# The feed-forward part on two 64-row TensorE tiles, with fences and block ends ordered by hand

## The chip, the cores and the metric

The kernel runs on one core of a Trainium2 chip. The metric is the device time of one execution in microseconds (us). A core has a matrix engine (TensorE, "PE" in the profile, with its weight loads as "PEld"), a vector engine (VectorE, "DVE"), an engine for activation functions (ScalarE, "ACT"), GpSimd ("POOL") and a queue engine that issues most transfers (SyncE, "SP"). They run side by side and wait for one another through semaphores. TensorE writes only to PSUM, eight banks of 128 partitions by 512 fp32 values here; ScalarE and VectorE read the results from there.

## What is computed

Inputs are bf16. There are 2048 tokens of width D = 576. A layernorm of x feeds two branches: a sliding-block attention (32 query heads, 16 key and value heads of width 128, the last 512 cached positions), and a mixer with a feed-forward network of width F = 4608. Cut to what matters:

```python
def _B_ref(x, w1, w2, w3, w4):
    h = _gelu(_layernorm(x, axis=-1) @ w1)
    ...
    hs = jnp.concatenate([g0, g1, g2, g3], axis=-1) @ w2
    x1 = x + hs
    h2 = _gelu(_layernorm(x1, axis=-1) @ w3) @ w4
    return x1 + h2

x = A_x
xn = _layernorm(x, axis=-1)
s = _A_ref(xn, A_k_cache, A_v_cache, A_wq, A_wo)
g = _silu(_B_ref(xn, B_w1, B_w2, B_w3, B_w4))
return x + s * g
```

The change touches the line of `h2` (the feed-forward part): `w3` is 576 x 4608, `w4` is 4608 x 576.

## The kernel before

Tokens are taken in NB = 4 blocks of QB = 512, each of TB = 4 row tiles of 128. The first part of the program (up to line 657) does the attention and the mixer for all blocks and leaves s and x1 in DRAM scratch. The second part, from line 660, is the feed-forward network; the layernorm of x1 for a block (`ln3_steps`, line 164) writes `xm_b`, and four DMA transposes (`ln3_transpose`, line 168) bring it, as `xT_b`, into the form that a matmul streams.

Weights are loaded once, in nine slices (`load_w`, line 679): `w3_s` with five chunks of 128 rows for the contraction over D = 4 x 128 + 64 (the fifth chunk holds 64 rows of weights and 64 of zeros, set by a memset on GpSimd, line 682), and `w4_s`. All of these loads stand on SP's queue, three for a slice, ahead of the loads of s and x (`load_sx`, line 694).

F is cut into FC = 36 columns of 128, called fc. `up(b, fc)` (line 703) runs five matmuls of 512 streamed columns, one for each chunk of D, into one PSUM bank `ph`, and a gelu on ScalarE (line 711) makes the bf16 tile `h3` of it. `down(fc, tt)` (line 714) multiplies one 128-token piece of `h3` with `w4`: 512 columns into the bank `pm[tt]` (line 717) and the last 64 into `pr` (line 718). PSUM has three banks for `ph`, four for `pm` and one for `pr`, which all four row tiles share.

Blocks 0 to 2 run ups and downs in turn, the downs LA = 3 fc behind the ups (loop at line 760). After the last down of a block, `finish` (line 721) adds x1 on VectorE (line 731), takes a tanh on ScalarE (line 733), forms out and g with four more VectorE operations (lines 735, 736, 738, 741) and stores them. Block 3 runs all its ups first, then the downs of one row tile after the other, the last of them in three cuts of columns (line 786), so that little is left behind the last matmul.

In this part the order on every engine comes from a scheduler that follows the program's order and priorities; only in the first part are SP, GpSimd and TensorE ordered by hand (`tc.manual_schedule`). Waits between engines and for the reuse of a buffer are placed automatically.

Of the kernel before, what the change touches and what calls it, by code (L numbers as in the profile page):

```python
# [8 lines left out]
P = 128  # L9
# [6 lines left out]
SP = mybir.EngineType.SP  # L16
POOL = mybir.EngineType.Pool
PE = mybir.EngineType.PE

LN_EPS = 1e-5  # L20
GELU_A = 0.7978845608028654
# [8 lines left out]
def kernel(  # L30
# [14 lines left out]
    nc = tc.nc  # L45
# [72 lines left out]
        nc.scalar.activation(out=e[:], in_=y[:, 0:1], func=ACT.Exp, scale=0.0)  # L118
        return y

    def layernorm_steps(pool, dsts, srcs, rsqrt=rsqrt_newton):
        n = len(srcs)
        hw = D // 2
        st_ = {}

        def stats(i):
            if i == 0:
                st_["mv"] = pool.tile([P, n, 2], FP32, name="ln_mv")
            st = pool.tile([P, 2, 6], FP32, name="ln_st")
            for j in range(2):  # L130
                tc.keep_in_program_order(
                    nc.vector.bn_stats(out=st[:, j, :], in_=srcs[i][:, j * hw:(j + 1) * hw]))
            nc.vector.bn_aggr(out=st_["mv"][:, i, :], in_=st[:])

        def inv():
            st_["r"] = rsqrt(pool, st_["mv"][:, :, 1], n)

        def apply(i):
            nc.vector.tensor_scalar(out=dsts[i], in0=srcs[i], scalar1=st_["mv"][:, i, 0:1],
                                    scalar2=st_["r"][:, i:i + 1], op0=ALU.subtract, op1=ALU.mult)  # L140

        return ([lambda i=i: stats(i) for i in range(n)] + [inv] + [lambda i=i: apply(i) for i in range(n)])

# [15 lines left out]
    def load_x1(b):  # L159
        x1 = x1_pool.tile([P, TB, D], BF16, name="x1")  # L160
        nc.sync.dma_start(out=x1[:], in_=rows(x1_dram, b * TB, TB))
        x1_t[b] = x1

    def ln3_steps(b):
        xm = xm_b[b % 2]
        return layernorm_steps(small, [xm[:, tt, 0:D] for tt in range(TB)], [x1_t[b][:, tt, :] for tt in range(TB)])

    def ln3_transpose(b):
        for tt in range(TB):
# [2 lines left out]
    with ExitStack() as actx:  # L172
        def pool(name, bufs, space=None):
            kw = {} if space is None else {"space": space}
            return actx.enter_context(tc.tile_pool(name=name, bufs=bufs, **kw))
# [484 lines left out]
    with ExitStack() as bctx:  # L660
# [4 lines left out]
        res = pool("b_res", 1)  # L665
        WS = 4
        NSL = FC // WS
        w3_s, w4_s = [], []
        for i in range(NSL):
            w3_s.append(res.tile([P, NDC, WS * P], BF16, name=f"w3_s{i}"))  # L670
            w4_s.append(res.tile([P, WS, D], BF16, name=f"w4_s{i}"))
        h3_pool = pool("h3_pool", 6)
        hl_pool = pool("hl_pool", FC)
        fin = pool("fin", 2)
        sx_pool = pool("sx_pool", 2)
        ps_h3 = pool("ps_h3", 3, PSUM)
        ps_h2 = pool("ps_h2", 1, PSUM)

        def load_w(i):
            w3, w4 = w3_s[i], w4_s[i]  # L680
            c0 = i * WS * P
            nc.gpsimd.memset(w3[DR:, NF, :], 0.0)
            nc.sync.dma_start(out=w3[:, 0:NF, :],
                              in_=B_w3[0:NF * P, c0:c0 + WS * P].rearrange("(kc p) f -> p kc f", p=P))
            nc.sync.dma_start(out=w3[0:DR, NF, :], in_=B_w3[NF * P:D, c0:c0 + WS * P])
            nc.sync.dma_start(out=w4[:], in_=B_w4[c0:c0 + WS * P, :].rearrange("(fc p) d -> p fc d", p=P))

        with tc.issue_after(last_t[0].ins):
            for i in range(NSL):
# [4 lines left out]
        def load_sx(b):  # L694
            s_b = sx_pool.tile([P, TB, D], BF16, name="s_b")
            nc.sync.dma_start(out=s_b[:], in_=rows(s_dram, b * TB, TB))
            x_b = sx_pool.tile([P, TB, D], BF16, name="x_b")
            nc.sync.dma_start(out=x_b[:], in_=rows(x2, b * TB, TB))
            sx_t[b] = (s_b, x_b)

        h3_t = {}

        def up(b, fc, hp):
            ph = ps_h3.tile([P, QB], FP32, name="ph3", tag="h3")
            w3 = w3_s[fc // WS]
            f0 = (fc % WS) * P
            for kc in range(NDC):
                nc.tensor.matmul(ph[:, :], lhsT=w3[:, kc, f0:f0 + P], rhs=xT_b[b % 2][:, kc, :],  # L708
                                 start=(kc == 0), stop=(kc == NDC - 1))
            h3 = hp.tile([P, QB], BF16, name="h3")  # L710
            nc.scalar.activation(out=h3[:, :], in_=ph[:, :], func=ACT.Gelu_apprx_tanh)  # L711
            h3_t[fc] = h3

        def down(pm, pr, fc, tt):
            w4 = w4_s[fc // WS]
            lhsT = h3_t[fc][:, tt * P:(tt + 1) * P]
            nc.tensor.matmul(pm[tt][:, :], lhsT=lhsT, rhs=w4[:, fc % WS, 0:M0], start=(fc == 0), stop=(fc == FC - 1))  # L717
            nc.tensor.matmul(pr[:, tt, :], lhsT=lhsT, rhs=w4[:, fc % WS, M0:D],  # L718
                             start=(fc == 0 and tt == 0), stop=(fc == FC - 1), skip_group_check=True)

        def finish(b, tt, parts):
            t = b * TB + tt
            s_b, x_b = sx_t[b]
            o = fin.tile([P, D], BF16, name="o")
            g2 = fin.tile([P, D], BF16, name="g2")

            def part(ps, lo, hi):
                n = hi - lo
                bs = fin.tile([P, n], FP32, name="bs")
                for src, l0, l1 in ps:  # L730
                    nc.vector.tensor_tensor(out=bs[:, l0 - lo:l1 - lo], in0=src, in1=x1_t[b][:, tt, l0:l1], op=ALU.add)  # L731
                th = fin.tile([P, n], FP32, name="th")
                nc.scalar.activation(out=th[:], in_=bs[:], func=ACT.Tanh, scale=0.5)
                t1 = fin.tile([P, n], FP32, name="t1")
                nc.vector.tensor_tensor(out=t1[:], in0=bs[:], in1=s_b[:, tt, lo:hi], op=ALU.mult)
                nc.vector.scalar_tensor_tensor(out=o[:, lo:hi], in0=th[:], scalar=1.0, in1=t1[:], op0=ALU.add,
                                               op1=ALU.mult)
                nc.vector.tensor_tensor(out=o[:, lo:hi], in0=o[:, lo:hi], in1=x_b[:, tt, lo:hi], op=ALU.add)
                if hi == D:
                    nc.sync.dma_start(out=out2[t * P:(t + 1) * P, :], in_=o[:])  # L740
                nc.vector.scalar_tensor_tensor(out=g2[:, lo:hi], in0=th[:], scalar=1.0, in1=bs[:], op0=ALU.add,
                                               op1=ALU.mult)
                if hi == D:
                    nc.scalar.dma_start(out=g_dram[t * P:(t + 1) * P, :], in_=g2[:])

            for ps, lo, hi in parts:
                part(ps, lo, hi)
            return part

        LA = 3  # L750
        for b in range(NB):
            load_sx(b)
            lastb = b == NB - 1
            if not lastb:
                load_x1(b + 1)
            pm = [ps_h2.tile([P, M0], FP32, name=f"pm{tt}") for tt in range(TB)]
            pr = ps_h2.tile([P, TB, R0], FP32, name="pr")
            whole = lambda tt: [([(pm[tt][:, :], 0, M0), (pr[:, tt, :], M0, D)], 0, D)]
            if not lastb:
                for step in range(FC + LA):  # L760
                    if step < FC:
                        up(b, step, h3_pool)
                    if step == 8:
                        for fn in ln3_steps(b + 1):
                            fn()
                        ln3_transpose(b + 1)
                    if step >= LA:
                        for tt in range(TB):
                            down(pm, pr, step - LA, tt)
                for tt in range(TB):  # L770
                    finish(b, tt, whole(tt))
            else:
                for fc in range(FC):
                    up(b, fc, hl_pool)
                for tt in range(TB - 1):
                    for fc in range(FC):
                        down(pm, pr, fc, tt)
                    finish(b, tt, whole(tt))
                tt = TB - 1
                part = finish(b, tt, [])  # L780
                cuts = [0, 288, 480, D]
                for i in range(3):
                    lo, hi = cuts[i], cuts[i + 1]
                    ps = pm[TB - 1 - i][:, 0:hi - lo]
                    for fc in range(FC):
                        nc.tensor.matmul(ps, lhsT=h3_t[fc][:, tt * P:(tt + 1) * P],
                                         rhs=w4_s[fc // WS][:, fc % WS, lo:hi], start=(fc == 0), stop=(fc == FC - 1))
                    part([(ps, lo, hi)], lo, hi)


    flag = nc.values_load(flag_i[0:1, 0:1])
# [121 lines left out]
```

## Time and profile before

| what | value |
|---|---|
| median of 9 runs (lowest to highest) | 864.57 us (860.73 to 868.32) |
| the profiled execution | 863.79 us |
| its span, first to last instruction | 862.0 us |
| feed-forward part, first to last matmul | 558.15 to 855.4 us |
| mean granted TensorE clock | 0.996 |
| gelu, 128x512, one | 597 ns |
| VectorE step over 128x576 in fp32 (lines 735, 736, 741), one | 750 ns |

The profile is one execution. A "group" is all instructions of one line, engine and operation; its row has the count, the busy time, the mean duration of one, then the idle time of the engine just before them and what ended it. A matmul's duration runs from its start to the modelled arrival of its last result, so that consecutive ones overlap: the distance between two starts tells what one costs in a dense stream. In a timeline a row has the start, the length and the number of merged instructions.

### The profile page before, as it was taken

Reading aid. Unit: us, or ns where it says so; the run is one execution under the profiler, and the core shown is the slowest. Engines: PE = TensorE matmul, PEld = TensorE weight load, DVE = VectorE, ACT = ScalarE, POOL = GpSimd, SP = SyncE. Lnnn points to the kernel's source line nnn. Section 1 sums busy time; section 2 is a strip of 40 time slices with the busy share of each in tenths; the row PEclk is TensorE's granted clock in tenths of the full one; section 3 lists DMA queues with packets and bytes.
Section 4 is the critical chain, followed back from the end, with each engine's and each line's share of the span. In section 5 each row is a group of like instructions: output and inputs, shape, how many; then the busy total and the mean of one; then the engine's idle time right before and its main releaser. Section 6 shows DMA issues by size and latency. Waiting matters only on the chain.

```text
span 862.0 us, 16356 instructions
## 1 busy us (share of the span) xinstructions
PE 846.5 (98%) x6540; PEld 474.5 (55%) x6540; DVE 390.7 (45%) x1210; ACT 457.7 (53%) x819; POOL 81.0 (9%) x143
## 2 busy tenths in 40 slices
PE   8999899999999999999999999999999999999996
PEld 5665555665665665555566565544444444444455
DVE  5779731368851288871154875100063026005024
ACT  5776663598773498774378872132232333235510
POOL 3442101310100101010010102000000000000000
PEclk9999999999999999999999999999999999999999
DMA  7995751472461284272157337980023005001001
GB/s 177 248 239 136 151 92 40 133 134 60 113 109 46 61 129 92 73 151 53 13 97 153 86 73 190 329 246 1 1 84 86 1 8 154 8 1 56 1 14 45
DMA packets 138098, 83.74 MB, mean 97 GB/s; under 512 B 104496, under 2 KB 131376, under 8 KB 138016
## 3 DMA queue, kind: packets, MB, share of 16 engines
q1 hardware_dynamic: 126448, 51.24, 29.0%
q0 software_dynamic: 8448, 28.15, 11.4%
q10 hardware_dynamic: 3120, 3.25, 1.1%
q8 instruction: 53, 0.87, 0.4%
q14 instruction: 29, 0.24, 0.1%
HBM read 49.17 MB, written 9.44 MB: 68 GB/s over the span
## 4 chain that ended last, share of the span: by engine, by line


## 5 line engine op out<-in xcount | busy, mean ns | idle before, releaser
L365 ACT ACTIVATE pT<-sc 128x512 bf16<-128x512 f32 x512 | 289.4, 596 | 104.7 <-PE sc L363 97.5
L363 PE MATMUL sc<-qT,kT 128*128 128x512 bf16 x512 | 183.1, 380 | 0.8 <-DVE qT L353 0.6
L708 PE MATMUL ph<-xT_b,w_s 128*128 128x512 bf16 x720 | 172.1, 379 | 0.0
L380 PEld LDWEIGHTS <-pT 128*128 128x128 bf16 x2048 | 140.1, 98 | 54.2 <-DVE o L385 3.7
L711 ACT ACTIVATE h<-ph 128x512 bf16<-128x512 f32 x144 | 85.6, 597 | 155.5 <-PE ph L708 150.9
L380 PE MATMUL po<-v_sb,pT 128*128 128x129 bf16 x2048 | 162.4, 221 | 2.7 <-DVE o L385 2.5
L348 PE MATMUL psq<-xT_b,wq_b 128*128 128x512 bf16 x640 | 159.2, 379 | 2.3 <-DMA xT_b<-xn_b 2.0
L717 PE MATMUL pm<-w_s,h 128*128 128x512 bf16 x540 | 145.8, 380 | 0.0
L731 DVE TENSOR_TENSOR bs<-pm,x 128x512 f32<-128x512 f32 (+3 forms) x18 | 11.1, 629 | 243.5 <-PE pm L717 195.6
L404 PE MATMUL pswo<-wo_sb,oT 128*128 128x512 bf16 x512 | 116.5, 379 | 0.0
L384 DVE RECIPROCAL ri<-po 128x2 f32<-128x2 f32 x256 | 42.7, 167 | 159.6 <-PE po L380 156.4
L385 DVE TENSOR_TENSOR o<-po,ri 128x256 bf16<-128x256 f32 x256 | 107.7, 421 | 11.0 <-DMA oT<-o 5.0
L348 PEld LDWEIGHTS <-wq_b 128*128 128x128 bf16 x640 | 62.5, 98 | 76.2 <-issue 4.1
L708 PEld LDWEIGHTS <-w_s 128*128 128x128 bf16 x720 | 63.8, 98 | 73.4
L718 PE MATMUL pr<-w_s,h 128*128 128x64 bf16 x540 | 99.1, 193 | 0.0
L404 PEld LDWEIGHTS <-oT 128*128 128x128 bf16 x1024 | 65.0, 98 | 55.2
L717 PEld LDWEIGHTS <-h 128*128 128x128 bf16 x540 | 52.7, 98 | 63.8 <-issue 0.6
L355 ACT ACTIVATE qT<-psq 128x512 bf16<-128x512 f32 x96 | 57.4, 598 | 29.3 <-PE psq L348 29.3
L363 PEld LDWEIGHTS <-kT 128*128 128x128 bf16 x512 | 47.6, 98 | 28.5 <-DVE qT L353 1.2
L718 PEld LDWEIGHTS <-h 128*128 128x128 bf16 x540 | 51.0, 98 | 12.2 <-issue 0.4
L220 POOL DMA_DIRECT2D wq_b<-in_A_wq_dram x30 | 23.4, 780 | 312.5 <-PE psq L348 237.2
L414 ACT ACTIVATE s_out<-pswo 128x512 bf16<-128x512 f32 x16 | 9.6, 597 | 48.2 <-PE pswo L404 40.3
(99 smaller groups left out, 510.1 us busy)
## 6 DMA issues: line engine op xcount, KB each, us to landing
wq_b<-in_A_wq_dram POOLq DMA_DIRECT2D x30, 512.0 KB, 5.4
w_s<-in_B_w_dram SPq DMA_DIRECT2D x9, 576.0 KB, 8.3
wo_sb<-in_A_wo_dram POOLq DMA_DIRECT2D x8, 576.0 KB, 4.7
w_s<-in_B_w_dram SPq DMA_DIRECT2D x9, 512.0 KB, 9.3
x_dram<-x SPq DMA_DIRECT2D x4, 576.0 KB, 3.5
x<-x_dram SPq DMA_DIRECT2D x4, 576.0 KB, 4.4
s_b<-s_dram SPq DMA_DIRECT2D x4, 576.0 KB, 6.0
x_b<-in_A_x_dram SPq DMA_DIRECT2D x4, 576.0 KB, 6.0
```

The costliest lines, as they stand in the source:

```text
L348: nc.tensor.matmul(psq[:, :], lhsT=w[:, kc, hh * Dh:(hh + 1) * Dh], rhs=xT_b[qb % 2][:, kc, :], start=(kc == 0), stop=(kc == NDC - 1))
L355: nc.scalar.activation(out=qT[:, :], in_=psq[:, :], func=ACT.Copy)
L363: nc.tensor.matmul(sc[:, :], lhsT=kT[:, g, kc * P:(kc + 1) * P], rhs=qT_t[u][:, :], start=True, stop=True)
L365: nc.scalar.activation(out=pT[:, :], in_=sc[:, :], func=ACT.Exp, scale=SCALE)
L380: nc.tensor.matmul(po[:, j, :], lhsT=pTs[kc][:, tt * P:(tt + 1) * P], rhs=v_sb[:, g, kc, 0:Dh + 1], start=(kc == 0), stop=(kc == KCH - 1))
L384: nc.vector.reciprocal(out=ri[:], in_=po[:, :, Dh])
L385: nc.vector.tensor_tensor(out=o[:, t0:t0 + 2, :], in0=po[:, :, 0:Dh], in1=ri[:].unsqueeze(2).to_broadcast([P, 2, Dh]), op=ALU.mult)
L404: nc.tensor.matmul(ps, lhsT=oT_t[qb * Hq + h][:, tt, :], rhs=wo_sb[:, h, lo:hi], start=(h == 0), stop=(h == Hq - 1))
L708: nc.tensor.matmul(ph[:, :], lhsT=w3[:, kc, f0:f0 + P], rhs=xT_b[b % 2][:, kc, :], start=(kc == 0), stop=(kc == NDC - 1))
L711: nc.scalar.activation(out=h3[:, :], in_=ph[:, :], func=ACT.Gelu_apprx_tanh)
L717: nc.tensor.matmul(pm[tt][:, :], lhsT=lhsT, rhs=w4[:, fc % WS, 0:M0], start=(fc == 0), stop=(fc == FC - 1))
L718: nc.tensor.matmul(pr[:, tt, :], lhsT=lhsT, rhs=w4[:, fc % WS, M0:D], start=(fc == 0 and tt == 0), stop=(fc == FC - 1), skip_group_check=True)
```

## The change

The feed-forward part is written anew; of the first part only the last layernorm differs.

- The contraction is cut into halves of 64 rows. Every matmul of the ups and of the downs in blocks 0 to 2 uses either partitions 0 to 63 (LO) or 64 to 127 (HI) of both operands. LO and HI are issued in turn, and write different banks.
- `up(g)` makes two fc at a time, in two banks. Its first half has five LO matmuls into bank 0 and five HI matmuls into bank 1, its second half four LO into bank 1 and four HI into bank 0. The ninth half chunk of w3 stands in a tile of its own, `w3r_s`: even fc in partitions 0 to 63, odd fc in 64 to 127. So that both halves find the same 64 rows of xT, the layernorm writes columns 512 to 575 twice (`twice=True`).
- `down(d, turn, js)` does two fc. In turn 0 LO works on row tiles 0 and 1 while HI works on 2 and 3; in turn 1 they are swapped. `pr` now takes two banks, one for LO and one for HI, `ph` two.
- Between the turns a `fence`, an operation of VectorE on one element of each of two banks, keeps LO and HI from writing the same bank at once.
- PE, VectorE and ScalarE are ordered by hand. Between any two down runs stands half of an up. Layernorm and output steps of VectorE are taken from a list, `work`, one after each run.
- At a block's end the results are moved out of PSUM into `bs` by ScalarE copies and VectorE adds, with half of an up between two half runs of downs. Where an up's second half comes there, the gelu of its second bank reads a VectorE copy (`split`).
- Block 3 runs its remaining ups over three pairs of banks in rotation, and then its downs over the full 128 rows, as before.
- g is stored through SP's queue in blocks 0 to 2, before through ScalarE's. Weight loads are four for a slice, and the memset of zero rows is gone.

```diff
+            parts = [(dsts[i], srcs[i])]
+            if twice:
+                parts = [(dsts[i][:, 0:D], srcs[i]), (dsts[i][:, D:DP], srcs[i][:, NF * P:D])]
...
-            nc.gpsimd.memset(w3[DR:, NF, :], 0.0)
...
+            last = B_w3[NF * P:D, c0:c0 + WS * P].rearrange("p (j two m) -> p j two m", two=2, m=P)
+            for k in range(2):
+                nc.sync.dma_start(out=w3r_s[i][k * DR:(k + 1) * DR, :, :], in_=last[:, :, k, :])
...
-        ps_h3 = pool("ps_h3", 3, PSUM)
+        ps_h3 = pool("ps_h3", 2, PSUM)
...
+        def fence(lo, hi):
+            f = fence_pool.tile([1, 1], FP32, name="fence")
+            nc.vector.tensor_scalar(out=f[:, :], in0=lo[0:1, 0:1], scalar1=hi[0:1, 0:1], scalar2=None, op0=ALU.add)
...
+            def first():
+                for kc in range(NDC):
+                    for i, half in enumerate((LO, HI)):
+                        mm(i, half, kc, kc == 0, False)
+
+            def second(split):
+                for kc in range(NF):
+                    for i, half in ((1, LO), (0, HI)):
+                        mm(i, half, kc, False, kc == NF - 1)
+                for i in range(2):
+                    src = ps[i]
+                    if i and split:
+                        src = hx_pool.tile([P, QB], FP32, name="hx")
+                        nc.vector.tensor_copy(out=src[:, :], in_=ps[i][:, :])
+                    h3 = h3_pool.tile([P, QB], BF16, name="h3")
+                    nc.scalar.activation(out=h3[:, :], in_=src[:, :], func=ACT.Gelu_apprx_tanh)
...
+            for i, j in js:
+                tts = (j, 2 + j) if turn == 0 else (2 + j, j)
+                for k, half in enumerate((LO, HI)):
+                    mm(pm[tts[k]][:, :], tts[k], fc0 + i, tts[k], half, 0, M0)
+                for k, half in enumerate((LO, HI)):
+                    mm(pr[k][:, tts[k], :], ("r", k), fc0 + i, tts[k], half, M0, D)
...
+        with tc.manual_schedule(engines={PE, DVE, ACTE}):
+            ups = [up(0, h3_banks()), up(1, bank_pair(["pr0", "pr1"]))]
...
+            for d in range(ND):
...
+                up_half()
+
+                down(d, 0, [(0, j), (1, j), (0, 1 - j), (1, 1 - j)] if i == 0 else
+                     [(0, j), (0, 1 - j), (1, j), (1, 1 - j)])
+                j = 1 - j
+                fence(pm[j], pm[2 + j])
+                pop()
+                if i < NP - 1:
+                    up_half()
+                    down(d, 1, [(0, j), (0, 1 - j), (1, j), (1, 1 - j)])
+                    j = 1 - j
+                    fence(pm[2 + j], pm[j])
+                    continue
+                assert not work
+                up_half(half[0] is not None)
...
+                down(d, 1, [(0, j), (1, j)])
+                nc.scalar.activation(out=bs[:, j, 0:M0], in_=pm[j][:, :], func=ACT.Copy)
+                add(2 + j, pm[2 + j][:, :])
+                up_half(half[0] is not None)
+                down(d, 1, [(0, 1 - j), (1, 1 - j)])
+                nc.scalar.activation(out=bs[:, 1 - j, 0:M0], in_=pm[1 - j][:, :], func=ACT.Copy)
+                for k, src in enumerate((x1, bs)):
+                    nc.vector.tensor_tensor(out=bs[:, :, M0:D], in0=pr[k], in1=src[:, :, M0:D], op=ALU.add)
+                add(3 - j, pm[3 - j][:, :])
...
+            sets = [[f"pm{j}", f"pm{2 + j}"], [f"pm{1 - j}", f"pm{3 - j}"], None]
...
+            for i in range(NPT - g + 1):
+                nxt = None
+                if g < NPT:
+                    nxt = up(g, bank_pair(sets[i % 3]) if sets[i % 3] else h3_banks())
+                    g += 1
+                    nxt[0]()
+                    nxt[2]()
+                    pop()
+                pend[1](False)
+                pop()
+                pend = nxt
```

`up` returns its two halves and its fence; `up_half` issues the first half of the next up together with its fence, or the second half of the one begun, and then one step of `work` (`pop`).

## The prediction

> **What bounds the kernel now.** I read the page's busy shares first, then the strip of slices, then the groups of the feed-forward lines, one window over the feed-forward part, and last its timeline.
>
> ```profile
> PE 846.5 (98%) x6540; PEld 474.5 (55%) x6540; DVE 390.7 (45%) x1210; ACT 457.7 (53%) x819; POOL 81.0 (9%) x143
> ...
> PE   8999899999999999999999999999999999999996
> ...
> L708 PE MATMUL ph<-xT_b,w_s 128*128 128x512 bf16 x720 | 172.1, 379 | 0.0
> ...
> L711 ACT ACTIVATE h<-ph 128x512 bf16<-128x512 f32 x144 | 85.6, 597 | 155.5 <-PE ph L708 150.9
> ...
> L717 PE MATMUL pm<-w_s,h 128*128 128x512 bf16 x540 | 145.8, 380 | 0.0
> ...
> L718 PE MATMUL pr<-w_s,h 128*128 128x64 bf16 x540 | 99.1, 193 | 0.0
> ```
>
> TensorE is busy in every slice, and in the feed-forward part it never waits: the idle figure of its three groups is 0.0, while ScalarE waits 150.9 us for it. The mean durations overlap, so pitches are needed. The window over the feed-forward part (us, then busy time of PE, weight loads, VectorE, ScalarE, GpSimd) and its timeline give them:
>
> ```profile
> 558.15:855.40 297.25, 297.22 (x1914) 146.68 (x1910) 65.60 (x154) 96.99 (x163) 0.00 (x0) 1.00 0.18 52
> ```
>
> ```profile
> 560.61 1.58 ACT L711 ACTIVATE h<-ph 128x512 bf16<-128x512 f32 x3
> ...
> 566.80 0.19 PE L718 MATMUL pr<-w_s,h 128*128 128x64 bf16 x1
> 566.80 0.10 PEld L717 LDWEIGHTS <-h 128*128 128x128 bf16 x1
> 566.83 0.38 PE L717 MATMUL pm<-w_s,h 128*128 128x512 bf16 x1
> ...
> 567.57 1.24 PE L708 MATMUL ph<-xT_b,w_s 128*128 128x512 bf16 x5
> 568.43 0.10 PEld L717 LDWEIGHTS <-h 128*128 128x128 bf16 x1
> 568.65 0.38 PE L717 MATMUL pm<-w_s,h 128*128 128x512 bf16 x1
> ...
> 568.91 0.60 ACT L711 ACTIVATE h<-ph 128x512 bf16<-128x512 f32 x1 [1.52 <-PE ph L708]
> ```
>
> Five ups stand between 567.57 and 568.65, so a 512-wide matmul takes 0.216 us of the stream; a narrow one takes 0.03 (566.80 to 566.83). Check: 720 x 0.216 + 540 x 0.246 + the last rows' 108 narrow ones (about 9.1) = 297.5 against 297.25 measured. The part is matmul stream without a hole, block ends included. Whatever the change saves in streamed columns it can keep only if it adds no wait to TensorE.
>
> **What the Trainium skill says.** "TensorE: Matmul & The Clock Gate", Part 3 (Packing small matmuls), says that matmuls on different row groups run at once, and gives 3.07 times for four row tiles; no run here shows a tile of fewer than 128 rows. The same page, "LDWEIGHTS", says that a weight load costs by its columns, not its rows: a half-height load would not be half price. The trace shows 128-column loads ready again after 0.03 us (566.80, next matmul 566.83). Its Part 2 says that matmuls start and end in program order, so that one held by a semaphore holds all behind it. "TensorEngine Tiling (Array Packing)", Restrictions (PSUM Pressure), says that two row tiles may not write one PSUM bank at the same time; hence the change's fences and swapped turns.
>
> **The change part by part.** The forecast is made against the profiled execution: 863.79 us, span 862.0; the median of the runs is 864.57, 0.8 above it.
>
> Ups. D = 576 is four chunks of 128 rows and one of 64, and before the fifth matmul streams 512 columns for half-filled rows. After, two up columns (fc) share nine half-height pairs: five in the first half, four in the second. Per pair of fc that is 9 x 0.216 = 1.944 us in place of 10 x 0.216 = 2.16; 72 pairs save 72 x 0.216 = 15.5 us. This holds if two half tiles really stream side by side at 0.216.
>
> Downs of blocks 0 to 2. For each (fc, row tile) one full pair (0.216 + 0.03) becomes two half-height pairs that run beside another row tile's; the stream time is the same, 0.246 for each of the eight in a pair of fc, but loads and matmuls double: eight instructions in 0.246 us, four of them loads. If loads are pulled forward past a waiting matmul, nothing is lost. If everything issues strictly in order, the load for the next wide LO matmul waits until the narrow HI one has started, about 0.027 later: 0.273. I take 0.25, and keep 0.246 and 0.273 as ends. A down run (four of them) is then 1.0 us.
>
> The new wait. TensorE's order is first half of an up, down run, second half, down run, first half of the next up. The ups have two banks (three before), since pr now needs two, and both are finished by the second half at the same moment. Both must be emptied by ScalarE, one after the other, before the next first half may write them; in the built order its first two matmuls each wait for ScalarE. Only one down run lies between. The chain: from the end of the stream (568.65) to the start of the gelu (568.91) 0.26; pitch of gelus back to back (1.58 - 0.597)/2 = 0.49; the second one's length 0.597; ScalarE to TensorE about 0.07, an estimate from VectorE to ScalarE in the last rows, where bs ends at 855.82 and th starts at 855.91. Sum 1.42 against 1.0 of cover: 0.42 us of wait. The LO tile may run one matmul ahead in it, but then stands behind HI's in program order, so I give nothing back for that. The loop has 54 pairs of fc in blocks 0 to 2: period 1.944 + 1.0 + 1.42 = 4.364 against 2.16 + 8 x 0.246 = 4.128 before, +0.236 each, +12.7 us (this includes the saving of 54 ups). The other 18 pairs, in the start and in the up-only part of block 3, save 18 x 0.216 = 3.9; there three bank pairs rotate, so nothing waits.
>
> Fences. A 1x1 VectorE operation after each run, three for a pair of fc, each estimated at 0.17 (the 128x4 form takes 0.162). TensorE waits for a fence only after another run has been issued: 0.26 + 0.17 + 0.07 = 0.5 against 0.86 or more. VectorE's hand order puts at most two work steps (0.75 each at the most) behind a fence, ahead of the next; by the runs' lengths they end before the next fence is due. Cost nothing; if a step ran late by one length, TensorE would lose up to 0.4 there. The layernorm's second apply (128x64, about 0.2, sixteen in all) and the tanhs go the same way: behind the two gelus on ScalarE.
>
> Block ends (three). Before, they cost TensorE nothing. Now the downs of the next block wait until ScalarE and VectorE have copied pm and pr; a split gelu through a VectorE copy (0.63 to 0.68) shortens one wait. Down half-runs are 0.5 long, the chain there is 0.26 + 0.65 + 0.07 = 0.98, so about 0.5 waits, and some 0.3 at the last pm bank; less the wait already counted, 0.35 each: 1.0 us.
>
> Start and end. The first up must still see the table load end (560.61); two ups' worth of matmuls (3.9 us) stand before the first wait, which costs 0.4, at the second pr bank. The last block's full-height downs start in pm0, one of the two banks that the very last up used: 0.26 + 0.6 + 0.07 = 0.9 of wait. Two changes of tiling, unmeasured, from nothing to 0.3 each: 0.3 together. Sum with the block ends 2.6.
>
> DMA. Nine more weight loads stand on SP ahead of the loads of s and x; at 0.5 to 1.5 us of issue each they end 5 to 13 us later, but s and x are needed only at the first block end, some 70 us on, and the x1 of block 1 stands ahead of the weights. The transposes of block 1 come after them and have until the same point. The g stores of blocks 0 to 2 go from ScalarE's queue to SP's, where only loads for the next block wait behind them. GpSimd's nine memsets go. Nothing on the path.
>
> Sum: +12.7 - 3.9 + 2.6 = +11.4 us. From the median, 864.6 + 11.4 = 876.
>
> **The rivals.**
> Faster: the gelus don't hold the ups. For it: ScalarE is busy for only 97 of 297 us, and the wait exists only because of where bank reuse falls. Then -15.5 + 2.6 + up to 2 of loads gives 850 to 854. Against it: each term of the 1.42 us chain is measured save the last. The sum is zero at a wait of 0.21 us for each pair of fc (54 x 0.024 = 1.3), so 0.21 of the 1.42 us would have to be wrong; a wait about that long gives no change, 864.6.
>
> Much slower: the doubled weight loads bind. No row shows a load of 64 rows. If such a load kept its port for 0.098 us, the length of a record, four would take 0.39 in place of 0.246, a down run 1.57; it would cover the gelus, and the period would be 1.944 + 3.14 = 5.08: +51 - 3.9 + 2.6 gives 914. At half of that excess (0.32 a pair, run 1.28) the period is 1.944 + 1.28 + 1.42 = 4.64: 891.
>
> The change doesn't do what it says: half tiles run one after the other, and the ups alone cost 72 x 1.944 = 140 us more: above 1000. The skill's row-tile figure is against it.
>
> **How the numbers follow.** Gelu wait, loads hidden or nearly so: 0.6, 868 to 886 (with loads at 0.273 it is 864.6 + 54 x 0.328 - 1.3 = 881; with a chain of 1.3 it is 869). Loads bind: 0.16, 887 to 915. Half tiles in turn: 0.02. Faster: 0.16, 850 to 861. No change, that is within 0.3% (2.6 us, about what a measurement can tell): 0.06. The range must leave out no more than 0.2: 859 takes the upper end of the faster case, 896 half of the loads' case. Faster 0.16, same 0.06, slower 0.78.
>
> **What would show it.** The group of ups should show TensorE idle some 20 us, released by ScalarE's gelu, once in each pair of fc, 0.3 to 0.5 each. The distance between first halves should be about 4.36 us, between two half-height ups in the up-only part 1.94. Down runs longer than 1.1 us would mean that loads bind. A long idle before the swapped matmuls, released by VectorE, would mean late fences. If TensorE shows no wait for ScalarE in the loop, the forecast is wrong in its main term.

## The result and the profile after

| | before | after |
|---|---|---|
| median of the runs | 864.82 us (55 runs) | 872.51 us (18 runs) |
| ratio | 1 | 1.0083, 95% interval 1.0061 to 1.0106 |
| profiled execution | 863.79 us | 881.60 us |
| feed-forward part, first matmul to the end of the last | 297.25 us | 304.75 us |

The kernel became 0.8% slower, about 7.2 us of 864.6. The medians are over all runs; the ratio leaves out those more than 1.5% above the fastest of their kernel. The profiled execution after is longer than its median; most of its extra time lies in the attention part, which ends at 568.3 us in it and at 558.2 before, although only the last layernorm differs there. In the profiles of the variants below, whose attention part is that of the kernel after, it ends anywhere between 556.7 and 570.5 us. So the feed-forward part is compared, in which TensorE's granted clock is 1.00 in every profile, and its 7.5 us more agree with the ratio.

The page of the kernel after, its busy shares and the groups that answer to those shown of before:

```profile
PE 848.8 (96%) x7980; PEld 509.0 (58%) x7980; DVE 433.5 (49%) x1401; ACT 453.7 (52%) x825; POOL 76.6 (9%) x134
...
PE   8999989999999998999999999999999999999996
...
L736 PE MATMUL ph<-xT_b,w_s 64*128 64x512 bf16 x976 | 154.4, 376 | 5.8 <-DVE hx L752 0.4
L754 ACT ACTIVATE h<-ph 128x512 bf16<-128x512 f32 x118 | 64.2, 594 | 167.2 <-PE ph L736 138.7
L773 PE MATMUL pm<-w_s,h 64*128 64x512 bf16 x864 | 140.6, 377 | 0.6 <-DVE fence L726 0.6
```

A busy share of 96% hides the loss: two half tiles run side by side here, and while HI waits the record of an LO matmul still covers much of the gap. The up group has 5.8 us of idle, not the 19 that the timeline below puts on it (54 x 0.35). The waits of the weight loads in the same profile point to the place, with no releaser named (us in total, times, longest):

```profile
PEld L736 <- issue: 16.2, 54, 0.5
```

There are 54 such waits, one in nearly every one of the 54 pairs of fc of blocks 0 to 2. The timeline of one period shows what happens (start, length, instruction):

```profile
605.66 1.08 ACT L754 ACTIVATE h<-ph 128x512 bf16<-128x512 f32 x2 [3.17 <-PE ph L736]
...
606.31 0.37 PE L736 MATMUL ph<-xT_b,w_s 64*128 64x512 bf16 x1
606.41 0.19 PE L773 MATMUL pr<-w_s,h 64*128 64x64 bf16 x1
606.61 0.21 DVE L726 TENSOR_SCALAR fence<-pm,pm 1x1 f32<-1x1 f32 x1 [1.64 <-PE pm L773]
606.79 1.02 PE L736 MATMUL ph<-xT_b,w_s 64*128 64x512 bf16 x7
607.46 0.57 PE L736 MATMUL ph<-xT_b,w3r_s 64*128 64x512 bf16 x2
607.67 0.57 PE L773 MATMUL pm<-w_s,h 64*128 64x512 bf16 x2
607.89 0.19 PE L773 MATMUL pr<-w_s,h 64*128 64x64 bf16 x1
607.92 0.38 PE L773 MATMUL pm<-w_s,h 64*128 64x512 bf16 x1
608.07 0.21 DVE L726 TENSOR_SCALAR fence<-ph,ph 1x1 f32<-1x1 f32 x1 [1.25 <-PE ph L736]
608.09 0.19 PE L773 MATMUL pr<-w_s,h 64*128 64x64 bf16 x1
...
609.91 1.09 ACT L754 ACTIVATE h<-ph 128x512 bf16<-128x512 f32 x2 [3.17 <-PE ph L736]
```

HI's last narrow matmul of the down run starts at 606.41 and would be done 0.03 later, at 606.44. LO has begun the next up at 606.31, in the bank that the first gelu has left. HI's first matmul, the head of a row of seven, starts only at 606.79, 0.05 after the second gelu's end (605.66 + 1.08 = 606.74). So HI loses 0.35 us, and from gelu to gelu (605.66 to 609.91) a pair of fc takes 4.25 us; before, two fc took 4.12 (two gelus 2.06 apart). Where no down run lies between, in the up-only part of block 3, the same ups follow one another every 1.94 us: the half tiles do stream side by side, 9 x 0.216 = 1.944.

The lines from 607.67 on show one thing more: LO leads HI by 0.20 us through the whole down run (first narrow matmuls at 607.89 and 608.09). A record does not name its half; they are told apart by the program's order within each half. LO's second wide matmul starts at 607.92, HI's first narrow one at 608.09, though the program has the latter first; that much holds whichever half is whose.

### The profile page after: what moved, and what is told of

Read it like the earlier page. It is cut to its first block, busy times and chain, and to the rows that moved or that the text cites. A ratio compares the mean times of both kernels' runs of the same rounds, so it can differ in the third digit from the quotient of the medians.

```text
span 879.8 us, 19509 instructions
## 1 busy us (share of the span) xinstructions
PE 848.8 (96%) x7980; PEld 509.0 (58%) x7980; DVE 433.5 (49%) x1401; ACT 453.7 (52%) x825; POOL 76.6 (9%) x134
## 4 chain that ended last, share of the span: by engine, by line
## 5 line engine op out<-in xcount | busy, mean ns | idle before, releaser
L736 PE MATMUL ph<-xT_b,w_s 64*128 64x512 bf16 x976 | 154.4, 376 | 5.8 <-DVE hx L752 0.4
L754 ACT ACTIVATE h<-ph 128x512 bf16<-128x512 f32 x118 | 64.2, 594 | 167.2 <-PE ph L736 138.7
L773 PE MATMUL pm<-w_s,h 64*128 64x512 bf16 x864 | 140.6, 377 | 0.6 <-DVE fence L726 0.6
L773 PE MATMUL pr<-w_s,h 64*128 64x64 bf16 x864 | 115.8, 189 | 0.2 <-ACT h L754 0.2
L773 PEld LDWEIGHTS <-h 64*128 64x128 bf16 x1728 | 87.2, 94 | 48.5 <-issue 2.5
L736 PEld LDWEIGHTS <-w_s 64*128 64x128 bf16 x1152 | 76.5, 94 | 53.4 <-issue 16.2
L726 DVE TENSOR_SCALAR fence<-pm,pm 1x1 f32<-1x1 f32 x115 | 23.8, 207 | 95.7 <-PE pm L773 86.7
L726 DVE TENSOR_SCALAR fence<-ph,ph 1x1 f32<-1x1 f32 x61 | 12.8, 210 | 92.4 <-PE ph L736 92.3
L937 PE MATMUL pm<-w_s,h 128*128 128x512 bf16 (+3 forms) x216 | 35.8, 313 | 0.8 <-ACT h L754 0.8
```

What stands on the lines that cost most here:

```text
L726: nc.vector.tensor_scalar(out=f[:, :], in0=lo[0:1, 0:1], scalar1=hi[0:1, 0:1], scalar2=None, op0=ALU.add)
L736: nc.tensor.matmul(ps[i][:, :], lhsT=lhsT, rhs=xT[half, kc, :], start=first, stop=last, skip_group_check=True)
L754: nc.scalar.activation(out=h3[:, :], in_=src[:, :], func=ACT.Gelu_apprx_tanh)
L773: nc.tensor.matmul(out, lhsT=h3_t[b, fc][half, tt * P:(tt + 1) * P], rhs=w4_s[fc // WS][half, fc % WS, lo:hi], start=key not in started, s ...
```

## The experiments

Each variant is the kernel after with the edit shown. "Period" is the usual distance between the first gelus of two pairs of fc in the loop. Each ratio is against runs of the kernel before that were made in the same session.

| variant | period, us | feed-forward part, us | ratio to before, 95% interval |
|---|---|---|---|
| before | 4.12 | 297.25 | 1 |
| after | 4.25 | 304.75 | 1.0083 (1.0061 to 1.0106) |
| e1: second gelu reads a copy | 3.90 to 3.93 | 291.36 | 0.9956 (0.9933 to 0.9980) |
| e2: gelus exchanged | 4.06 | 296.31 | 1.0008 (0.9985 to 1.0031) |
| e3: each fence twice | 4.25 | 306.50 | 1.0106 (1.0074 to 1.0138) |
| e4: downs over 128 rows | 4.47 | 316.25 | 1.0238 (1.0172 to 1.0304) |
| e5: e1 and the last downs' banks | 3.90 to 3.93 | 288.86 | 0.9884 (0.9813 to 0.9954) |
| e6: e2 with fixed banks | 4.25 | 305.27 | 1.0081 (1.0047 to 1.0114) |
| e7: e5 and a shorter layernorm step | 3.90 to 3.93 | 285.77 | 0.9881 (0.9822 to 0.9940) |

**e1: the wait taken away.**

```diff
-                    half[0][1](split)
+                    half[0][1](True)
```

> In the loop the second gelu of every up reads a VectorE copy of its bank, as it already does at the block ends, so both banks are free about 0.20 + 0.69 + 0.05 = 0.94 us after the up's last matmul, inside the down run of 0.98. Theory (the wait for the second gelu, 0.34 us in each of some 54 pairs of fc, is what took the saving and more): the period falls from 4.25 to about 3.91 us, the time by about 17 us, from 872.5 to about 855, ratio to the kernel before about 0.99. Rival (the loss lies in the half-height downs and their doubled weight loads, or in fences): the wait only moves, the period stays above 4.15 and the time above 867. Second rival (VectorE becomes too busy and its fences come late): the period lands between, 4.0 to 4.2, with TensorE waiting for fences.

The period fell as the theory said. The timeline of this variant shows why:

```profile
604.08 0.60 ACT L754 ACTIVATE h<-ph 128x512 bf16<-128x512 f32 x1 [2.54 <-PE ph L736]
...
604.11 0.69 DVE L752 COPY hx<-ph 128x512 f32<-128x512 f32 x1 [0.73 <-PE ph L736]
...
604.84 0.63 ACT L754 ACTIVATE h<-hx 128x512 bf16<-128x512 f32 x1 [0.16 <-DVE hx L752]
604.86 1.04 PE L736 MATMUL ph<-xT_b,w_s 64*128 64x512 bf16 x8
```

Both banks are read at the same time and free at about 604.8; the next up starts at 604.86, at the end of its down run, with both tiles in step. The feed-forward part fell by 13.4 us and the time, by the two ratios, by about 11, for 17 expected: five periods grew to between 4.5 and 5.3 us. VectorE now carries a copy for every pair of fc in the loop, and the part of the second rival that concerns single late steps is right (e7).

**e2: the two gelus exchanged, and e6: the same with fixed banks.**

```diff
-                for i in range(2):
+                for i in ((0, 1) if split else (1, 0)):
```

> The two gelus of an up in the loop change places: bank 1 is emptied first, bank 0 second. Theory (the HI tile carries the loop, and the LO tile's head start of one matmul during the wait is worth nothing): now LO's first matmul waits and HI's stands behind it, both start at the end of the second gelu, HI no later than before; period 4.25 us, time within 2.6 us of 872.5. Rival (the head start gives back part of the wait): it is lost here, up to 0.2 us in each of 54 pairs of fc, 11 us, about 883.

Neither theory's number came: the period was 4.06, shorter than 4.25 by 0.19, and no difference from the time before could be measured any longer. The timeline of e2:

```profile
606.64 0.57 PE L773 MATMUL pm<-w_s,h 64*128 64x512 bf16 x2
606.84 1.08 ACT L754 ACTIVATE h<-ph 128x512 bf16<-128x512 f32 x2 [2.97 <-PE ph L736]
...
607.62 0.38 PE L736 MATMUL ph<-xT_b,w_s 64*128 64x512 bf16 x1
607.79 0.19 PE L773 MATMUL pr<-w_s,h 64*128 64x64 bf16 x1
607.98 1.02 PE L736 MATMUL ph<-xT_b,w_s 64*128 64x512 bf16 x7
```

LO finishes the up at 606.64 and goes on to its downs; HI is 0.20 behind. The first gelu now reads the bank that LO wrote last, and starts at 606.84, while in the kernel after it had to wait for HI. HI is held from 607.79 + 0.03 to 607.98, 0.16 us in place of 0.35. I had expected LO to wait for the second gelu (606.84 + 1.08 = 607.92), but it starts at 607.62. A reason would be that the pool hands buffers on in the order in which they come free, so that the two banks change roles from one up to the next and LO always gets the first. If that is right, fixing the roles must undo the gain:

```diff
-        ps_h3 = pool("ps_h3", 2, PSUM)
+        ps_h3 = pool("ps_h3", 1, PSUM)
...
-            return [ps_h3.tile([P, QB], FP32, name="ph3", tag="h3") for _ in range(2)]
+            return [ps_h3.tile([P, QB], FP32, name=f"ph3{k}", tag=f"h3{k}") for k in range(2)]
```

> As the exchanged gelus, but each of the two up banks keeps its part: bank 0 is always written by LO first, then HI, and is emptied second. Theory (the exchange helped because buffers are handed on in the order in which they come free, so that LO still began in the bank that was free first, kept its lead of one matmul, and the first gelu could start at LO's end): with fixed banks LO must wait for the second gelu, HI stands behind it, no lead arises, and the period is 4.25 us again, time within 3 us of 872.5 (ratio about 1.008). Rival (it is the order of the gelus alone that saves 0.19 us): the period stays at 4.06, ratio about 1.001.

It did: 4.25 again, ratio 1.0081. In its timeline the tiles go in step, two records to a line, and both stand before the up:

```profile
611.84 0.21 PE L773 MATMUL pr<-w_s,h 64*128 64x64 bf16 x2
612.22 1.04 PE L736 MATMUL ph<-xT_b,w_s 64*128 64x512 bf16 x8 [0.17 <-ACT h L754]
```

The down run ends at 611.84 + 0.03, the up begins at 612.22: 0.35 us, the chain less its cover, now with no lead at all. So a lead of one tile is real; it is worth 0.19 us a pair of fc, if the first reader takes the leading tile's bank.

**e3: fences doubled.**

```diff
-            nc.vector.tensor_scalar(out=f[:, :], in0=lo[0:1, 0:1], scalar1=hi[0:1, 0:1], scalar2=None, op0=ALU.add)
+            for _ in range(2):
+                nc.vector.tensor_scalar(out=f[:, :], in0=lo[0:1, 0:1], scalar1=hi[0:1, 0:1], scalar2=None, op0=ALU.add)
```

> Every fence is issued twice. Theory (fences end well inside the run that covers them: 0.26 + 0.21 + 0.07 us against 0.86 or more): period unchanged at 4.25 us, time within 2.6 us of 872.5. Rival (TensorE waits for fences, hidden among the other waits): each of some 160 fences in the loop adds 0.1 to 0.2 us, 16 to 32 us, 888 to 905.

The period stayed at 4.25. The part grew by 1.75 us, most of it in two periods (5.11 for 4.41, 5.20 for 4.71) in which VectorE works through the layernorm's inverse square root. Fences cost nothing in the regular period, as forecast; they are near their limit only behind that one step. The ratio's interval overlaps that of the kernel after.

**e4: downs over the full 128 rows in the loop.** The fences after down runs go, and pr needs one bank.

```diff
-                tts = (j, 2 + j) if turn == 0 else (2 + j, j)
...
+                tt = j if turn == 0 else 2 + j
+                mm(pm[tt][:, :], tt, fc0 + i, tt, slice(0, P), 0, M0)
+                mm(pr[0][:, tt, :], ("r", 0), fc0 + i, tt, slice(0, P), M0, D)
...
-                for k, src in enumerate((x1, bs)):
+                for k, src in ((0, x1),):
```

> The downs of the loop use all 128 rows again, the first run of a pair of fc row tiles 0 and 1, the second 2 and 3; the ups stay half-height, the fences after down runs and the second pr bank's use go. So TensorE changes its tiling four times in a pair of fc. Theory: the streams are as long as before (0.246 us for each pair of a wide and a narrow matmul), so only the changes of tiling count; the one seen in the profile, from the end of the attention part to the first up, took about 0.1 us. Four of 0.1, one of them inside the wait for the gelu, make the period 4.25 + 0.3 = 4.55 us and the time about 889. If changes are free, 872.5. Rival (half-height downs are themselves dearer than full ones, by their doubled loads): full-height downs make the period less than 4.2 us and the time less than 868.

The period is 4.47, against 4.55 expected and 4.25. A change of tiling can be read off this variant's timeline:

```profile
607.73 0.19 PE L773 MATMUL pr<-w_s,h 128*128 128x64 bf16 x1
607.85 1.04 PE L736 MATMUL ph<-xT_b,w_s 64*128 64x512 bf16 x8
608.82 0.39 PE L773 MATMUL pm<-w_s,h 128*128 128x512 bf16 x1
```

The narrow matmul is through at 607.73 + 0.03; the first half-height one starts 0.09 later. Its four pairs take 0.86, to 608.71; the first full-height one starts 0.11 later. Four changes in a pair of fc then cost 0.40, but the period grew by only 0.22. Two of them lengthen the cover of the gelus, and the wait that is left shrinks by about 0.2. The rival, that half-height downs are dearer, falls: each of the eight half-height pairs in a pair of fc streams in the same 0.246 us (607.67 to 607.92 above) as a full one.

**e5: the last downs.** The kernel after waits at the turn from ups to last downs, and then twice where the narrow matmuls of the next row tile stand behind VectorE's read of the shared pr bank:

```profile
835.86 0.38 PE L937 MATMUL pm<-w_s,h 128*128 128x512 bf16 x1 [0.80 <-ACT h L754]
...
845.72 0.19 PE L937 MATMUL pr<-w_s,h 128*128 128x64 bf16 x1 [0.67 <-DVE bs L943]
```

Before, the waits for pr did not exist. The scheduler had let five wide matmuls of the next row tile pass, as the timeline of the kernel before shows:

```profile
828.66 1.24 PE L717 MATMUL pm<-w_s,h 128*128 128x512 bf16 x5
828.84 0.69 DVE L731 TENSOR_TENSOR bs<-pm,x 128x512 f32<-128x512 f32 x1 [35.73 <-PE pr L718]
829.44 0.21 DVE L731 TENSOR_TENSOR bs<-pr,x 128x64 f32<-128x64 f32 x1
829.69 0.76 DVE L735 TENSOR_TENSOR t<-bs,s_b 128x576 f32<-128x576 f32 x1
829.74 0.31 PE L718 MATMUL pr<-w_s,h 128*128 128x64 bf16 x5
```

```diff
-            pr = pr[0]
+            pm[0] = ps_h3.tile([P, QB], FP32, name="ph3", tag="h3")
...
-                    down128(pr[:, tt, :], fc, tt, M0, D, fc == 0 and tt == 0)
+                    down128(pr[tt % 2][:, tt, :], fc, tt, M0, D, fc == 0 and tt < 2)
```

> The always split gelu, and two edits to the last downs: row tile 0 is summed in a bank of the up pair that no late gelu reads, and the narrow sums of row tiles 0 to 2 take the two pr banks in turn. Theory (the idle 0.95 us at the turn to the last downs and the two waits of 0.67 us of narrow matmuls for VectorE's read of pr are lost time of the change): the feed-forward part falls from 291.2 to about 289 us, the ratio to the kernel before from 0.9956 to about 0.993. Rival (the hand order there is covered by other work): no change, 291.

288.86 us, 2.5 less than e1. The theory holds in the feed-forward part; the ratio's interval is too wide to show such a step by itself.

**e7: the layernorm's long step.** The timeline of e1 has eleven operations from 570.81 to the copy that they delay, of which the last two:

```profile
572.79 0.16 DVE L111 SCALAR_TENSOR_TENSOR nr_y<-nr_t,nr_y 128x4 f32<-128x4 f32 x1
572.87 0.69 DVE L752 COPY hx<-ph 128x512 f32<-128x512 f32 x1
```

```diff
+        return [begin, newton, newton, newton]
...
-        return ([lambda i=i: stats(i) for i in range(n)] + [inv] + [lambda i=i: apply(i) for i in range(n)])
+        mid = rsqrt_steps(pool, st_, n) if fine else [inv]
+        return ([lambda i=i: stats(i) for i in range(n)] + mid + [lambda i=i: apply(i) for i in range(n)])
```

> As the split gelu with both edits to the last downs, and the inverse square root of the next block's layernorm (eleven VectorE operations, 2.2 us in one step between two fences) is cut into four steps. Theory (that step makes a fence or a copy late once in each of blocks 0 to 2, 1.3, 1.1 and 0.95 us in the periods 5.28, 5.03 and 4.88 where others take 3.9): another 2.5 to 3.3 us less, the feed-forward part about 286 us, ratio about 0.990. Rival (more steps push others to the block ends, where TensorE waits for them): no gain over the kernel without the cut.

285.77 us; the periods of 5.28, 5.02 and 4.88 became 3.93, 4.08 and 3.93. Its ratio of 0.9881 has an interval that lies below 1, so it is faster than the kernel before, and with e5 it is the fastest of those tried; between these two the timed runs do not decide, the feed-forward part does.

## Why the prediction was right

The forecast was slower, 11.4 us more; measured were about 7.2 (5.3 to 9.2 by the interval). Its main mechanism, ScalarE emptying two banks one after the other behind a cover of one down run, is shown by e1 (without it the loss turns into a gain) and by the 54 waits. The sum came nearer than its terms did: the loop cost about 6 us less than forecast, the terms outside it about 2 us more, and these partly cancel. By its steps:

- Saving of the ups: 1.944 us forecast for a pair of fc, 1.94 measured. Right.
- Half-height downs: 0.25 forecast, 0.246 measured. The doubled loads are hidden, and the rival in which they bind is out, by the timeline and by e4.
- The chain of the gelus: this is the term that was too large. Forecast 1.42 us: 0.26 + 0.49 + 0.597 + 0.07. Measured from HI's end (606.44 less the down run of 0.98, 605.46) 0.20 + 1.08 + 0.05 = 1.33. The first term is taken up below the list. The last, 0.07, was estimated from two lines that are 0.09 apart (855.82 and 855.91); the loop shows 0.05. With the cover of 0.98 in place of 1.0 the wait is 0.35 for 0.42 and the period 4.25 for 4.364, 6 us less over 54 pairs.
- "so I give nothing back for that": the value was right for this kernel, the reason was not. I had the half tiles in step, held by program order; the timeline has LO 0.20 ahead until the next wait. Nothing came back because the first gelu reads the bank that HI, the late tile, wrote last. e2 got 0.19 of it back, e6 took it away again.
- Start, block ends and turn: 2.6 forecast. What is left of the measured 7.5 after the loop (54 x 0.13 = 7.0) and the other ups (-3.9) is 4.4. In it the turn is as forecast (0.9; 0.80 of it is named as a wait for the gelu); the two waits for pr, 1.3, were not foreseen. I had compared the last downs by their edits, which are few, and not by who orders them: the scheduler's five wide matmuls ahead were lost with it. About 0.6 more is the layernorm's inverse square root in one step, which the forecast put among steps of 0.75 at the most; it takes 2.2. The ten pairs with the later gelu make about 0.5. The rest, about 1, was not taken apart; the forecast had 1.4 for start and block ends.
- Fences at nothing: right in the regular period (e3), though one takes 0.21 us (606.61 above) and not the 0.17 estimated.
- Changes of tiling: 0.3 forecast for two, about 0.2 by the 0.09 and 0.11 of e4, one of them hidden in the turn's wait.
- The working on the faster rival put no change at a wait of 0.21 us. The kernel of e2 comes near to that, with a wait of 0.16 us and a ratio of 1.0008.

The first term of the chain, 0.26, is right for the gelu that I took it from (568.91), but it does not hold for the kernel after. In the kernel before, the gelu ahead of that one starts 0.20 after the end of its stream:

```profile
566.59 0.38 PE L717 MATMUL pm<-w_s,h 128*128 128x512 bf16 x1
566.79 0.60 ACT L711 ACTIVATE h<-ph 128x512 bf16<-128x512 f32 x1 [1.46 <-PE ph L708]
```

Where nothing else delays a gelu of the kernel before, it starts 0.20 after the stream up to the sixth and again in block 3, and 0.26 after it from the seventh to the end of block 2. The semaphore records of the trace tell the two kinds apart: those at 0.26 wait, besides TensorE, for ScalarE's own semaphore. The kernel before has six buffers for `h3` in blocks 0 to 2, so this extra wait begins where a buffer is used again. The kernel after has 36, and there only the gelus of ten pairs of fc have it, from the 37th gelu on. The first gelus of these pairs start 0.25 after the stream, and the regular periods among them are 4.30 us in place of 4.25:

```profile
639.67 1.08 ACT L754 ACTIVATE h<-ph 128x512 bf16<-128x512 f32 x2 [3.17 <-PE ph L736]
643.98 1.08 ACT L754 ACTIVATE h<-ph 128x512 bf16<-128x512 f32 x2 [3.22 <-PE ph L736]
648.28 0.60 ACT L754 ACTIVATE h<-ph 128x512 bf16<-128x512 f32 x1 [3.22 <-PE ph L736]
```

So the larger number of `h3` buffers, which the forecast did not price, is the likely reason that this term came out 0.06 shorter; no run changed it alone.

The Trainium skill, "TensorE: Matmul & The Clock Gate", Part 3, says that matmuls of different row groups overlap, and this case's traces agree (1.94 us for nine pairs). Its Part 2 says that matmuls stay in program order, and Part 3 adds that this holds for start and end. In their starts it does not hold here between two half tiles: 607.92 before 608.09. What does hold all that stands behind it is a matmul that waits for a semaphore: LO's second up matmul, ready at about 606.53, is not seen before 606.79. "TensorEngine Tiling (Array Packing)", Key Properties, says that a change of tiling drains the engine; e4 gives it a price of about 0.1 us.

## What to carry to other kernels

When a matrix engine has no holes, price a change that saves streamed columns by the buffers that it gives up: two results that are finished at the same moment and read one after the other need the sum of the two reads as cover, that is, as other work for the matrix engine meanwhile, and a second engine for one of them takes that away. Where an order is laid by hand in place of a scheduler's, list what the scheduler had moved ahead of each wait, since that is lost without any line of the diff saying so.

## What the runs showed of the hardware that I had not expected

Two half-height tiles need not be in step: the tile that got a start of one matmul kept it through a run of downs (LO's narrow matmul at 607.89, HI's at 608.09, 0.20 us apart), while doubled weight loads, four in 0.246 us, cost nothing. A change between 64-row and 128-row tiling took 0.09 us one way and 0.11 the other. A gelu started 0.20 us after the stream that it waited for, and 0.25 to 0.26 after it where it also waited for ScalarE's own semaphore.
